# Sums of w_out's blocks put together by transfers instead of VectorE additions

## The chip, the cores and the metric

One Trainium2 chip, one of its cores. The metric is the device time of one execution in microseconds, the median of the runs of one kernel. The core has five engines that run side by side, each through its own list of instructions in order: TensorE (PE; its weight loads are shown as PEld), VectorE (DVE), ScalarE (ACT), GpSimd (POOL) and SyncE (SP), which here only issues transfers. Engines wait for each other by semaphores. Transfers are carried out by 16 DMA engines.

## The reference

Linear attention for 8 batches of 8 heads, 576 tokens, 64 columns a head, and then a feed-forward layer with softplus, on 4608 tokens of 512 columns and 2048 hidden columns, in float32:

```
q_s = exp(q - max(q, -1));  q_s = q_s / (sum(q_s, -1) + 1e-9)
k_s = exp(k - max(k, 2));   k_s = k_s / (sum(k_s, 2) + 1e-9)
kv  = einsum('bhsd,bhse->bhde', k_s, v)
x   = einsum('bhsd,bhde->bhse', q_s, kv)      # heads side by side: 4608 x 512
h   = x @ w_in
g   = maximum(h, 0) + log1p(exp(-abs(h)))
out = g @ w_out
```

## The kernel before, in words

Tokens come in nine tiles of 512. The hidden columns come in 16 chunks of 128; chunk j holds 128 columns of w_in and the 128 rows of w_out that go with them. TensorE multiplies in a reduced float32, so each operand is kept as a high part and a low part and a product takes three matmuls (high by high, low by high, high by low). A chunk with both parts of both matrices is 1 MB in SBUF (`parts[j]`, lines 198 to 207); it is stored once to DRAM (`keep_w`) and fetched again where it is needed.

Tiles 0 to 2 are multiplied plainly, chunk by chunk: `up` (lines 595 to 597) makes 512 columns of h, ScalarE bends them, VectorE makes the low part of g (line 613), and `down` (lines 637 to 639) adds to the output. For tile 2 the 16 chunks are fetched one by one by `fetch_w` (line 224) into five buffers in turn (w0, spare, w2, w3, w15), each fetch released when TensorE has left the buffer's former chunk. Tiles 3 to 8 are multiplied in three pairs by a scheme of seven block products in place of eight. It needs sums and differences of blocks of w_in and w_out for each of eight pairs of chunks s = 0 to 7 (chunks 2s and 2s+1). Those of w_out are made by `sum_out_unit(s)` (lines 273 to 299), while tile 2 is being multiplied. Its first two steps, `whole_w(0)` and `whole_w(1)`, put a chunk's high and low part together again, 128 partitions by 512 columns each; steps 2 to 5 form the four combinations (line 283), steps 6 and 7 split them into high and low parts, step 8 stores 1 MB to DRAM.

In the same stretch of time the attention for later tiles goes on: per batch and group of heads the tile `kvt` with k and v is loaded by SP (lines 314 and 318) after GpSimd has set its edges (lines 310 to 313); VectorE takes the maximum along the tokens (line 336), GpSimd the maximum over the partitions (line 339), VectorE subtracts it (line 371), ScalarE takes the exponential, TensorE multiplies k and v (line 387). For a tile of q, VectorE makes the low part `q_lo` (line 529), which the products of lines 535 to 537 wait for.

The order of all work is written out by hand: `ORDER` is a list of short names, `do` carries out one after another, and each engine gets its instructions in that order. `y2.0` is step 0 of `sum_out_unit(2)`, `R0.4` fetches chunk 4, `n` loads the next k and v tile, `U36` and `O36` are up and down of tile 2 for chunk 4 (36 = 2 x 16 + 4). SP takes nearly all transfers, in one queue.

Of the kernel before, what the change touches and what calls it, by code (L numbers as in the profile page):

```python
# [16 lines left out]
ALU = mybir.AluOpType  # L17
# [31 lines left out]

STAGE = ("w1", "w15", "w0", "spare", "w5", "w6", "w7", "w8")  # L50
STAGE_OUT = ("w12", "w13", "w14", "w1", "w12", "w13", "x1", "w3")
ORDER = """
# [17 lines left out]
def tile_attn_ffn(  # L70
# [9 lines left out]
    nc = tc.nc  # L80
# [162 lines left out]
    def sum_unit(s):  # L243


        f = wp.tile([P, 2, 4, 2 * P], F32R, name=STAGE[s])
        y = f[:, 1].bitcast(F32)
# [25 lines left out]
    def sum_out_unit(s):  # L273

        f = (xp if STAGE_OUT[s][0] == "x" else wp).tile([P, 2, 4, 2 * P], F32R, name=STAGE_OUT[s])
        y = f[:, 1].bitcast(F32)

        def whole_w(z, engine=nc.vector):
            hi, lo = (parts[2 * s + z][:, i, 1].bitcast(F32) for i in range(2))
            engine.tensor_tensor(out=y[:, 2 * z:2 * z + 2].rearrange("p a n -> p (a n)"), in0=hi, in1=lo, op=ALU.add)  # L280

        def add(out, a, b, op, engine=nc.vector):
            engine.tensor_tensor(out=y[:, out], in0=y[:, a], in1=y[:, b], op=op)

        def high():
            nc.scalar.copy(f[:, 0], y)

        def low():
            nc.vector.tensor_tensor(out=f[:, 1], in0=y, in1=f[:, 0].bitcast(F32), op=ALU.subtract)

        def keep():
            kept_sums_out[s] = dram.tile([P, 2, 4, 2 * P], F32, name=f"sums_out{s}")
            nc.sync.dma_start(out=kept_sums_out[s], in_=f.bitcast(F32))

        return [
            lambda *e: whole_w(0, *e), lambda *e: whole_w(1, *e), lambda *e: add(3, 1, 3, ALU.add, *e),
            lambda *e: add(1, 0, 1, ALU.subtract, *e), lambda *e: add(0, 3, 0, ALU.subtract, *e),
            lambda *e: add(2, 2, 0, ALU.subtract, *e), high, low, keep,
        ]
# [797 lines left out]
```

## Time and profile before

| | us |
|---|---|
| median of 3 runs | 813.59 (813.24 to 814.54) |
| span of the profiled execution, first to last instruction | 811.1 |
| TensorE busy | 800.8 |
| VectorE busy | 625.9 |
| ScalarE busy | 536.3 |
| GpSimd busy | 115.1 |
| DMA queue of SP, share of the 16 engines' span | 67.3% |

The profile comes from one execution; of its time the page gives the span. "Busy" is the time in which an engine executes; its waits, and what released it, are listed apart. Shares over the whole span are averages over stages with different limits, so the rows below are taken from the stretch of time in which the changed instructions stand.

### The profile page before, as it was taken

To read this page: it belongs to the slowest core of one execution; us is meant where nothing else is said; L and a number is where in the kernel's file an instruction comes from. 1 tells how busy PE (TensorE), PEld (TensorE's weight loads), DVE (VectorE), ACT (ScalarE), POOL (GpSimd) and SP (SyncE) were. 2 spreads that over 40 slices of the span, in tenths; PEclk is the share of its full clock that TensorE was granted. 3 is DMA by queue.
4 is the path that set the end of the run, shared out by engine and by line. 5 is a ranking of instruction groups with operands and counts; after the bars stand their busy time and mean duration, and the time that the engine had idled before them with its cause. 6 is when DMAs were issued, how large, how long until landed. Compare 5 with 4: busy or idle time off the path is not lost.

```text
span 811.1 us, 12147 instructions
## 1 busy us (share of the span) xinstructions
PE 800.8 (99%) x4244; PEld 656.6 (81%) x4244; DVE 625.9 (77%) x1027; ACT 536.3 (66%) x868; POOL 115.1 (14%) x219
## 2 busy tenths in 40 slices
PE   8999999999999999999999999999999999999997
PEld 7578888888877888888888888888888888888886
DVE  8888974569989999767889998767999922237983
ACT  4999974646777575778885765978657544445651
POOL 2320022000010100010100003440001350000044
PEclk9999999999999999999999999999999999999999
DMA  9974116749987998998497637982866695449654
GB/s 340 373 273 182 59 39 274 267 176 385 401 279 257 328 337 343 340 372 253 139 324 237 186 115 265 275 270 93 280 201 197 178 261 198 175 156 322 211 126 70
DMA packets 114493, 193.75 MB, mean 239 GB/s; under 512 B 8000, under 2 KB 90176, under 8 KB 104192
## 3 DMA queue, kind: packets, MB, share of 16 engines
q1 hardware_dynamic: 111168, 186.67, 67.3%
q0 software_dynamic: 2944, 6.04, 4.0%
q8 instruction: 34, 0.56, 0.3%
q10 hardware_dynamic: 320, 0.26, 0.1%
q14 instruction: 27, 0.22, 0.1%
HBM read 149.95 MB, written 42.99 MB: 238 GB/s over the span
## 4 chain that ended last, share of the span: by engine, by line
PE 92%; DVE 3%; issue 2%; DMA 2%; SPq 1%; ACT 0%; POOL 0%; DVEq 0%; ACTq 0%; POOLq 0%
PE po L722 6%; PE po L838 6%; PE po L836 6%; PE po L837 6%; PE po L724 6%; PE po L723 6%; PE ph L595 5%; PE po L637 5%; PE ph L597 5%; PE ph L596 5%; PE po L638 5%; PE po L639 5%; PE ph L722 3%; PE ph L724 3%; PE ph L723 3%; PE ph L836 3%
## 5 line engine op out<-in xcount | busy, mean ns | idle before, releaser
L881 POOL DMA_DIRECT2D out<-w x92 | 59.3, 653 | 305.7 <-DVE w L873 304.4
L816 ACT CAST g_hi<-w 128x512 fp32r<-128x512 f32 x74 | 46.2, 624 | 31.1 <-PE ph L837 8.0
L595 PE MATMUL ph<-x,w 128*128 128x512 f32 x164 | 65.3, 398 | 1.1 <-DMA w<-kept 1.1
L637 PE MATMUL po<-w,g_hi 128*128 128x512 f32 x164 | 64.5, 394 | 0.0
L596 PE MATMUL ph<-x,w 128*128 128x512 f32 x164 | 64.0, 390 | 0.0
L597 PE MATMUL ph<-x,w 128*128 128x512 f32 x164 | 64.0, 390 | 0.0
L639 PE MATMUL po<-w,g_lo 128*128 128x512 f32 x164 | 64.0, 390 | 0.0
L638 PE MATMUL po<-w,g_hi 128*128 128x512 f32 x164 | 63.9, 390 | 0.0
L819 DVE TENSOR_TENSOR g_lo<-w,g_hi 128x512 fp32r<-128x512 f32 x74 | 51.0, 690 | 16.0 <-ACT g_hi L816 12.6
L803 DVE TENSOR_TENSOR w<-w,w 128x512 f32<-128x512 f32 x72 | 49.2, 686 | 5.3 <-ACT w L756 5.2
L752 ACT ACTIVATE w<-w 128x512 f32<-128x512 f32 x48 | 30.1, 632 | 34.8 <-DVE w L745 18.9
L745 DVE TENSOR_TENSOR w<-po,w 128x512 f32<-128x512 f32 x24 | 16.6, 690 | 46.9 <-PE po L724 46.3
L816 ACT CAST w<-w 128x512 fp32r<-128x512 f32 x52 | 32.2, 623 | 25.1 <-DVE w L819 8.1
L604 ACT ACTIVATE g<-ph 128x512 f32<-128x512 f32 x48 | 28.6, 599 | 29.8 <-PE ph L597 26.7
L722 PE MATMUL po<-w,x 128*128 128x512 f32 x112 | 44.1, 394 | 0.0
L724 PE MATMUL po<-w,x 128*128 128x512 f32 x112 | 43.7, 390 | 0.0
L723 PE MATMUL po<-w,x 128*128 128x512 f32 x112 | 43.7, 390 | 0.0
L610 ACT CAST g_hi<-g 128x512 fp32r<-128x512 f32 x46 | 28.6, 621 | 21.2 <-PE po L638 20.7
L613 DVE TENSOR_TENSOR g_lo<-g,g_hi 128x512 fp32r<-128x512 f32 x46 | 31.4, 683 | 12.6 <-ACT g_hi L610 12.4
L339 POOL PARTITION_ALL_REDUCE mx<-mx x20 | 17.2, 860 | 160.6 <-DVE mx L336 133.0
L336 DVE TENSOR_REDUCE mx<-kvt 128x128 f32<-128x640 f32 x28 | 36.9, 1319 | 2.5 <-DMA kvt<-in_kv_tail 2.5
L819 DVE TENSOR_TENSOR w<-w,w 128x512 fp32r<-128x512 f32 x52 | 35.6, 689 | 3.1 <-ACT w L816 1.0
(392 smaller groups left out, 2381.8 us busy)
## 6 DMA issues: line engine op xcount, KB each, us to landing
x<-sums SPq DMA_DIRECT2D x24, 1024.0 KB, 5.2
kvt<-in_kv SPq DMA_DIRECT2D x30, 512.0 KB, 7.4
kept<-w SPq DMA_DIRECT2D x15, 1024.0 KB, 9.6
w<-kept SPq DMA_DIRECT2D x13, 1024.0 KB, 8.1
x<-sums_out SPq DMA_DIRECT2D x44, 256.0 KB, 4.9
w<-kept SPq DMA_DIRECT2D x36, 256.0 KB, 4.5
x<-kept SPq DMA_DIRECT2D x36, 256.0 KB, 4.5
w<-sums_out SPq DMA_DIRECT2D x36, 256.0 KB, 5.6
```

The source lines that it names most:

```text
L595: nc.tensor.matmul(ph, lhsT=w_hi, rhs=x_hi, start=h == 0, stop=False)
L596: nc.tensor.matmul(ph, lhsT=w_lo, rhs=x_hi, start=False, stop=False)
L597: nc.tensor.matmul(ph, lhsT=w_hi, rhs=x_lo, start=False, stop=h == HP - 1)
L637: nc.tensor.matmul(po, lhsT=g_hi[:, ms], rhs=w_hi, start=j == 0, stop=False)
L638: nc.tensor.matmul(po, lhsT=g_hi[:, ms], rhs=w_lo, start=False, stop=False)
L639: nc.tensor.matmul(po, lhsT=g_lo[:, ms], rhs=w_hi, start=False, stop=j == NJ - 1)
L722: nc.tensor.matmul(ph, lhsT=w_hi, rhs=x_hi, start=c == 0 and i in (0, 4), stop=False, **more)
L723: nc.tensor.matmul(ph, lhsT=w_lo, rhs=x_hi, start=False, stop=False, **more)
L724: nc.tensor.matmul(ph, lhsT=w_hi, rhs=x_lo, start=False, stop=c == 1, **more)
L816: nc.scalar.copy(ring[p, i, s][0], right_of(p, i, s))
L819: engine.tensor_tensor(out=lo, in0=right_of(p, i, s), in1=hi.bitcast(F32), op=ALU.subtract)
L836: nc.tensor.matmul(bank, lhsT=w_hi, rhs=hi, start=begin, stop=False, **more)
```

## The change

For s = 2 to 5 the two steps `whole_w(0)` and `whole_w(1)` no longer give VectorE an addition. SP issues a transfer that copies the high part (256 KB, from SBUF to SBUF) into the target, and GpSimd issues a transfer that adds the low part to it. The four pairs are s = 2, 3, 4 and 5, so eight additions of line 280 become eight copies and eight adding transfers. `ORDER` is the same. Lines behind line 50 have a number larger by 1 in the kernel after, and those behind the function's changed lines one larger by 6 (line 224 becomes 225, 280 becomes 286, 339 becomes 345).

```diff
 STAGE = ("w1", "w15", "w0", "spare", "w5", "w6", "w7", "w8")
+BY_DMA = (2, 3, 4, 5)
...
         def whole_w(z, engine=nc.vector):
             hi, lo = (parts[2 * s + z][:, i, 1].bitcast(F32) for i in range(2))
-            engine.tensor_tensor(out=y[:, 2 * z:2 * z + 2].rearrange("p a n -> p (a n)"), in0=hi, in1=lo, op=ALU.add)
+            total = y[:, 2 * z:2 * z + 2].rearrange("p a n -> p (a n)")
+            if s in BY_DMA:
+                nc.sync.dma_start(out=total, in_=hi)
+                nc.gpsimd.dma_start(out=total, in_=lo, accum_op=ALU.add)
+                return
+            engine.tensor_tensor(out=total, in0=hi, in1=lo, op=ALU.add)
```

SP's queue before, around the fetch of chunk 11 (`spare<-kept`); `sums` are stores of w_in's combinations, the fetch into `w_2755` is chunk 12, that into `w_2830` chunk 13:

```order
L265 DMA sums_2687<-w_1960 128x2048
L224 DMA spare<-kept_1876 128x2048
L265 DMA sums_2732<-w_1989 128x2048
L224 DMA w_2755<-kept_1904 128x2048
L314 DMA kvt<-in_kv 128x8x128
L318 DMA kvt<-in_kv_tail 64x2x128
L224 DMA w_2830<-kept_1664 128x2048
```

The same place after; `w_2712` is the target of pair 5, its first copy reads chunk 10 (`w_2645`) and its second chunk 11:

```order
L266 DMA sums_2693<-w_1960 128x2048
L283 DMA w_2712<-w_2645 128x512
L225 DMA spare<-kept_1876 128x2048
L266 DMA sums_2739<-w_1989 128x2048
L225 DMA w_2762<-kept_1904 128x2048
L283 DMA w_2712<-spare 128x512
L320 DMA kvt<-in_kv 128x8x128
L324 DMA kvt<-in_kv_tail 64x2x128
L225 DMA w_2838<-kept_1664 128x2048
```

The first copy of pair 5 stands ahead of the fetch of chunk 11, and the second ahead of the load of the next k and v tile and the fetch of chunk 13.

GpSimd before, where the edges of a k and v tile are set and two maxima over the partitions follow:

```order
L313 MEMSET kvt 128x10
L310 MEMSET kvt 64x2x64
L311 MEMSET kvt 64x2x65
L313 MEMSET kvt 128x10
L339 ISA mx<-mx 128x128 x2
```

GpSimd after, at the same place; the transfers are the adding ones of pair 2 (its second) and of pair 3 (its first):

```order
L284 DMA w_2284<-w_2297 128x512
L316 MEMSET kvt 64x2x64
L317 MEMSET kvt 64x2x65
L319 MEMSET kvt 128x10
L345 ISA mx<-mx 128x128
L284 DMA w_2430<-spare 128x512
L345 ISA mx<-mx 128x128
```

An adding transfer, which waits for its copy, now stands ahead of the tile's edges and of each of the two maxima.

GpSimd before, at the last maximum of this stretch:

```order
L313 MEMSET kvt 128x10
L339 ISA mx<-mx 128x128
L310 MEMSET kvt 64x2x64
L311 MEMSET kvt 64x2x65
L313 MEMSET kvt 128x10
```

GpSimd after, at the same place, with the last three adding transfers (of chunks 9, 10 and 11):

```order
L284 DMA w_2620<-w_2546 128x512
L284 DMA w_2712<-w_2645 128x512
L345 ISA mx<-mx 128x128
L284 DMA w_2712<-spare 128x512
L316 MEMSET kvt 64x2x64
L317 MEMSET kvt 64x2x65
L319 MEMSET kvt 128x10
```

Two of them stand ahead of the maximum, and the last one between it and the edges of the k and v tile that is loaded next.

## Rows read from the trace of the kernel before

**Rows 1.** The page: the span, and busy time of each engine
```profile
span 811.1 us, 12147 instructions
PE 800.8 (99%) x4244; PEld 656.6 (81%) x4244; DVE 625.9 (77%) x1027; ACT 536.3 (66%) x868; POOL 115.1 (14%) x219
```

**Rows 2.** TensorE's waits from 225 to 330 us: who for, us, times, longest
```profile
PE ph L595 <- DMA w<-kept: 1.1, 1, 1.1
PE att L535 <- DVE q_lo L529: 0.7, 1, 0.7
```

**Rows 3.** Busy time by stretch: PE, PEld, DVE, ACT, POOL, clock, DMA share, GB/s
```profile
240.00:262.00 22.00, 21.29 (x127) 17.50 (x124) 21.73 (x39) 17.46 (x32) 2.34 (x8) 1.00 0.76 245
262.00:290.00 28.00, 28.00 (x192) 22.83 (x192) 27.12 (x54) 17.61 (x28) 3.82 (x13) 1.00 0.95 341
290.00:314.00 24.00, 24.00 (x119) 20.32 (x118) 23.24 (x41) 18.13 (x32) 0.25 (x2) 1.00 0.98 348
314.00:340.00 26.00, 26.00 (x116) 21.55 (x115) 23.57 (x39) 15.66 (x25) 1.80 (x2) 1.00 0.85 309
```

**Rows 4.** Order of time on SP's queue: start, us, line, operation, target and source
```profile
239.63 0.33 SPq L224 DMA_DIRECT2D w<-kept  x1
243.89 0.33 SPq L224 DMA_DIRECT2D spare<-kept  x1
277.58 0.38 SPq L224 DMA_DIRECT2D spare<-kept  x1
289.15 0.55 SPq L314 DMA_DIRECT2D kvt<-in_kv  x1
303.37 0.56 SPq L224 DMA_DIRECT2D w<-kept  x1
```

**Rows 5.** Transfers issued at 239.63, 243.89, 277.58 and 303.37: KB each, us to landing
```profile
w<-kept SPq DMA_DIRECT2D x1, 1024.0 KB, 5.4
spare<-kept SPq DMA_DIRECT2D x1, 1024.0 KB, 6.4
spare<-kept SPq DMA_DIRECT2D x1, 1024.0 KB, 8.9
w<-kept SPq DMA_DIRECT2D x1, 1024.0 KB, 10.5
```

**Rows 6.** Order of time on TensorE at three places
```profile
256.25 0.36 PE L535 MATMUL att<-q_hi,kv_hi 128*128 128x192 f32 x1 [0.71 <-DVE q_lo L529]
289.50 0.50 PE L595 MATMUL ph<-x,spare 128*128 128x512 f32 x1
314.25 0.39 PE L595 MATMUL ph<-x,w 128*128 128x512 f32 x1
```

**Rows 7.** Line 280: duration ns least, median, most; first and last start
```profile
L280 DVE TENSOR_TENSOR w<-w x11: 628/686/693, 218.0 to 321.1; 128x512 f32<-128x512 f32 x11
```

**Rows 8.** Order of time on VectorE near 253 us
```profile
252.45 0.82 DVE L371 TENSOR_TENSOR kvt<-kvt,mx 128x640 f32<-128x640 f32 x1
253.79 0.68 DVE L280 TENSOR_TENSOR w<-spare 128x512 f32<-128x512 f32 x1
```

**Rows 9.** Line 881, GpSimd's transfers of 64 KB: duration ns
```profile
L881 POOL DMA_DIRECT2D out<-w x92: 648/648/974, 494.1 to 805.0; - x92
```

**Rows 10.** Order of time on GpSimd at two places
```profile
250.78 0.70 POOL L339 PARTITION_ALL_REDUCE mx<-mx  x1 [9.13 <-DVE mx L336]
289.20 0.20 POOL L310 MEMSET kvt<- 64x128 f32 x1 [5.76 <-ACT w L679]
```

**Rows 11.** Transfers from 262 to 314 us, GB/s in 40 slices; tails from 200 to 335
```profile
GB/s 277 403 240 334 365 337 126 338 403 246 378 339 360 404 353 347 290 334 429 441 422 231 273 246 341 355 332 390 391 315 309 246 378 447 429 429 410 388 320 361
DMA packets 7162, 17.88 MB, mean 344 GB/s; under 512 B 369, under 2 KB 4977, under 8 KB 5367
kvt<-in_kv_tail SPq DMA_DIRECT2D x8, 64.0 KB, 6.9
```

**Rows 12.** Transfers issued from 320 to 340 us
```profile
out<-w SPq DMA_DIRECT2D x4, 256.0 KB, 2.6
```

## The prediction

> **What bounds the kernel now.** I read the page first, then the waits of TensorE, then busy time by stretch, then the order of time on each engine around the changed instructions, and last the transfers. TensorE is busy 99% of a span of 811.1 us [rows 1], so an edit on another engine counts only where TensorE has to wait. Between 225 and 330 us, the stretch in which the sums of w_out's blocks are formed, it waited twice: 1.1 us for a chunk of weights and 0.7 us for VectorE's q_lo [rows 2]. The reader should then see how little room each helper has there. VectorE works 21.73 of 22 us, then 27.12 of 28 and 23.24 of 24; the 16 DMA engines have a share of 0.76 before 262 us, 0.95 until 290 and 0.98 until 314 [rows 3]. So two resources are nearly full beside a TensorE that is full: the change relieves one and loads the other.
>
> What links the DMA engines to TensorE is the stream of weight chunks for the third tile of tokens (the 16 fetches of line 224). The fetch of chunk 15 is issued at 303.37 [rows 4] and lands 10.5 us later [rows 5], at 313.87; TensorE takes the chunk at 314.25 [rows 6]. That is 0.4 us in hand. For chunk 11 the same views give 277.58 + 8.9 = 286.5 against 289.50, so 3.0 us. Chunk 15 is the tightest of the sixteen behind the changed instructions.
>
> **What goes from VectorE.** Eight additions, the 128x512 ones of line 280 that start between 241 and 287 us, at 0.686 us each [rows 7]; consecutive ones start 0.6 us apart, so 4.8 us of VectorE's time. It hides almost wholly, since TensorE waits for VectorE only at 256.25, for 0.71 us [rows 6]. Three removed additions stand before the q_lo it waits for, the last at 253.79 [rows 8], so the stall could vanish: at best -0.7 us. After 262 no wait is left to remove.
>
> **What comes to GpSimd.** Eight accumulating transfers, each standing in GpSimd's order where VectorE's addition stood. GpSimd's transfers cost it 0.65 us each [rows 9], 5 us in all; GpSimd is mostly idle. But each waits until its copy has landed, and behind it on the same engine stand the maxima over the partitions (line 339) and the clearing of the next k and v tile. Take the one before the maximum at 250.78 [rows 10]. Its copy waits for chunk 5, issued at 239.63 [rows 4] and landed 5.4 us later [rows 5], at 245.0; a copy more ahead of it makes that about 246. By then the fetch of chunk 6 is queued (issued 243.89), which landed after 6.4 us, at 250.3, and now lands about 1.2 later with a copy and an addition more ahead of it. Transfers of one queue land in their order here: a 64 KB tail takes 6.9 us [rows 11], longer than 256 KB behind little else, 2.6 us [rows 12]. So the copy lands near 252.3, the addition is issued, the clearing and the maximum (0.7 us) follow, and VectorE's subtraction, at 252.45 before [rows 8], starts near 254.3: 1.9 late, 1.3 after the 0.6 saved at 253.79. The q_lo comes 1.3 later and the stall becomes 2.0, not 0. This delay is not added below: a TensorE 1.3 us late at 256 still meets the same late weights at 314.
>
> **What comes to the DMA engines.** Sixteen transfers of 256 KB, two for each addition, 4.2 MB. The trace before has no copy from SBUF to SBUF and no adding transfer, so I bound the price. From 262 to 314 us 17.88 MB moved [rows 11] in about 50.1 us of busy share, 2.8 us per MB or 0.73 us for 262,144 bytes; the best slice there, 447 GB/s, gives 0.59. An adding transfer reads its target as well as its source, so at most twice 0.73. I take 0.65 for both kinds, between the two rates, because these are runs of 2 KB, and 4,977 of the 7,162 packets behind the mean are shorter. The ends stay 0.59 and, for the adding ones, 1.46.
>
> The Trainium skill (DMA: Bandwidth & Descriptors, "Rules for kernel authors") says of an accumulating transfer that it "reads its destination and writes it later". No row before shows one; by the rule the upper end, +10.1, gains weight.
>
> Which of the sixteen matter? Five (the copies of the first three additions and the first two adding transfers) fall before 262, where 0.24 of 22 us, 5.3 us, is free: absorbed. Eleven come after, five copies and six adding ones, all ahead of chunk 15 in time: 11 x 0.65 = 7.2 us. Free there: 0.05 x 28 + 0.02 x 24 = 1.9 us. With the 0.4 that chunk 15 has in hand, TensorE meets it late by 7.2 - 1.9 - 0.4 = 4.9 us. With the cheapest price and the adding transfers free of charge it is 5 x 0.59 - 2.3 = +0.7; with the dearest 5 x 0.73 + 6 x 1.46 - 2.3 = +10.1.
>
> The Trainium skill (DMA: Bandwidth & Descriptors, "Issuing engines are not separate DMA queues") states that transfers from all issuing engines run on the same 16 DMA engines. No transfer of GpSimd's falls into this stretch, so the trace is silent; by the rule all eleven count, and without it the adding ones might not: 5 x 0.65 - 2.3 = +1.0.
>
> **What comes to SP's queue.** Each copy also waits there for its chunk. The copy of chunk 10 now stands ahead of the fetch of chunk 11 and holds it until chunk 10 has landed: an estimate of 1 to 3 us after the 277.58 of before, against 3.0 in hand. This is part of the same lateness, not one more term.
>
> After 314 nothing gives the time back: TensorE is busy 26.00 of 26 us to 340 [rows 3], and later fetches are released by its own progress. So span 811.1 + 4.9 = 816.0. The profiled execution's span is 2.5 us under the median of the runs, 813.59; I take the same 2.5 around it: 818.5 us.
>
> **Rivals.**
> First, the cover holds, and it is not slower. For: chunk 11 has 3.0 us in hand, a VectorE that is ahead stores its sums earlier and clears the queue before chunk 15, and the transfers might overlap better than a mean rate says. It decides if the eleven transfers cost under 0.35 us each (11 x 0.35 - 2.3 = 1.6). Against: the share is 0.98 from 290 to 314. Time: 811.1 + 2.5 less 0.7 to plus 1.6, that is 812.9 to 815.2.
>
> Second, a convoy on GpSimd and SP in place of the DMA rate. The last copy waits for chunk 11 (288 to 290 by the shift above), lands behind chunk 12 at 293 to 295, its addition and then the clearing of the k and v tile follow (289.20 before [rows 10]), the load of that tile waits for the clearing, and chunk 13's fetch stands behind that load on SP. From that load (289.15 [rows 4]) to chunk 15's landing took 24.7 us at a share of 0.98, so a load at 295 to 297 puts the landing at 320 to 322: +6 to +8, 819.6 to 821.6. For: the order. Against: the late lulls let the queue catch up.
>
> Third, adding transfers at the double price: +10.1, 823.7. For: the addition must fetch two operands. Against: nothing shows that the engine's rate falls with it.
>
> Fourth, VectorE was a bound after all and the stall at 256 vanishes with no cost elsewhere: 812.9. A gain beyond 0.2% of 813.6, 1.6 us (which is also about what a measurement tells from no change), has no wait to come from: after 225 only 1.8 us of waits exist, and the larger, for weights, is not VectorE's.
>
> **How the numbers follow.** DMA rate, +2.5 to +6: 0.47. Convoy: 0.18. Double price: 0.07. Cover holds, within 1.6 us either way: 0.24. Faster by more: 0.04. So slower is 0.47 + 0.18 + 0.07 = 0.72, no change 0.24, faster 0.04. The likeliest case has its own range 816.1 to 819.6. The range to hold the time 8 times in 10 leaves out the double price, half of the convoy and the faster end: 812.9 to 822.
>
> **What would show it.** Right: new waits of TensorE at line 595 for the fetched chunks 11 to 15, the largest near 314 us; a DMA share at 1 from 262 on; 16 more transfers of 256 KB; VectorE waiting at its subtraction for GpSimd's maximum near 252. Wrong: fetches that land as before with chunk 15 in time (the price per transfer was far lower), or TensorE waiting for VectorE or for the product of k and v more than for weights (the convoy on GpSimd decides, not the rate).

## The result, and the profile after

The kernel after takes 825.33 us (median of 4 runs, 825.03 to 826.23), the kernel before, run beside it, 814.07 (813.24 to 814.95). The ratio is 1.0138 with a 95% interval of 1.0123 to 1.0152: 11.2 us slower, where +4.9 and 818.5 us were forecast and 822.0 was the end of the range. The direction was right, the size was not. Medians and ratios, here and below, leave out two executions far off all others, 1002.84 us of pair2 and 1633.52 us of the kernel before beside it.

The page after, against [rows 1]: the span is 12.3 us longer with the same matmuls, and the clock row, 9 from end to end before, has one slice at 8.

```profile
span 823.4 us, 12180 instructions
PE 806.1 (98%) x4244; PEld 660.2 (80%) x4244; DVE 621.3 (75%) x1019; ACT 536.7 (65%) x868; POOL 120.4 (15%) x227
PEclk9999999999999989999999999999999999999999
```

TensorE's waits from 225 to 330 us after, against [rows 2] (us, times, longest):

```profile
PE att L541 <- DVE q_lo L535: 7.5, 2, 4.0
PE att L393 <- ACT kvt L383: 1.9, 1, 1.9
PE ph L601 <- DMA w<-kept: 0.6, 1, 0.6
```

Before there were 1.8 us of waits, now there are 10.0. The wait for weights in these lists says nothing of the change. It stands at 233.89 us before (1.08) and at 233.20 us after (0.56), ahead of the first changed instruction:

```profile
233.89 0.47 PE L595 MATMUL ph<-x,w 128*128 128x512 f32 x1 [1.08 <-DMA w<-kept]
```

Behind it TensorE waits for no weights in either kernel, though the forecast rested on such a wait; what is new is q_lo and the exponentials of k. Busy time by stretch after, against [rows 3] (PE, PEld, DVE, ACT, POOL, granted clock, DMA share, GB/s), and then the two stretches that follow the long waits:

```profile
240.00:262.00 22.00, 18.05 (x86) 14.78 (x81) 17.03 (x30) 14.38 (x26) 5.22 (x11) 0.95 1.00 316
262.00:290.00 28.00, 28.00 (x159) 22.93 (x159) 20.51 (x37) 16.38 (x24) 4.25 (x10) 0.98 0.88 289
290.00:314.00 24.00, 18.56 (x108) 14.89 (x107) 17.41 (x38) 12.66 (x21) 3.38 (x9) 0.86 1.04 333
314.00:340.00 26.00, 26.00 (x122) 21.77 (x121) 24.87 (x44) 15.45 (x27) 0.00 (x0) 1.00 0.87 326
...
259.60:263.40 3.80, 3.80 (x12) 3.01 (x11) 3.80 (x7) 2.90 (x5) 0.70 (x1) 0.55 0.56 139
304.80:311.00 6.20, 6.16 (x18) 5.12 (x19) 6.19 (x9) 2.59 (x5) 1.83 (x7) 0.51 1.08 325
```

The loss stands in two places, 254 to 264 us and 292 to 311 us. After the two long waits for q_lo (the rows below) TensorE ran on at a granted clock of about half (the 1.2 of its two levels, 1.2 and 2.4 GHz): 3.80 x 0.45 + 6.20 x 0.49 = 4.7 us. With 10.0 - 1.8 = 8.2 us of waits that is 12.9, against 12.3 of the span. The same can be read from single rows of TensorE (start, us):

```profile
258.77 0.36 PE L541 MATMUL att<-q_hi,kv_hi 128*128 128x192 f32 x1 [3.95 <-DVE q_lo L535]
...
259.65 0.57 PE L601 MATMUL ph<-x,spare 128*128 128x512 f32 x1
260.01 0.63 PE L602 MATMUL ph<-x,spare 128*128 128x512 f32 x1
...
294.71 0.80 PE L393 MATMUL att<-kvt 128*64 128x65 f32 x20 [1.85 <-ACT kvt L383]
...
304.84 0.58 PE L541 MATMUL att<-q_hi,kv_hi 128*128 128x256 f32 x1 [3.50 <-DVE q_lo L535]
```

The wait of [rows 6] has grown from 0.71 to 3.95, and the matmuls behind it take 0.63 us where one took 0.39. Who was late is read backwards, first on VectorE, then on GpSimd, then on SP and its transfer. VectorE:

```profile
255.57 0.83 DVE L377 TENSOR_TENSOR kvt<-kvt,mx 128x640 f32<-128x640 f32 x1 [4.67 <-POOL mx L345]
258.04 0.68 DVE L535 TENSOR_TENSOR q_lo<-att,q_hi 128x512 fp32r<-128x512 f32 x1
293.05 0.83 DVE L377 TENSOR_TENSOR kvt<-kvt,mx 128x640 f32<-128x640 f32 x1 [2.78 <-POOL mx L345]
298.76 1.43 DVE L289 TENSOR_TENSOR w<-w 128x256 f32<-128x256 f32 x4 [1.93 <-DMA w<-w]
304.10 0.69 DVE L535 TENSOR_TENSOR q_lo<-att,q_hi 128x512 fp32r<-128x512 f32 x1
```

GpSimd, at the same two places (against [rows 10]):

```profile
253.43 0.86 POOL L284 DMA_DIRECT2D w<-w  x1 [9.28 <-ACT w L553]
...
254.82 0.71 POOL L345 PARTITION_ALL_REDUCE mx<-mx  x1
...
291.47 0.86 POOL L284 DMA_DIRECT2D w<-w  x1 [3.63 <-DMA w<-w]
292.05 0.97 POOL L345 PARTITION_ALL_REDUCE mx<-mx  x1
```

And SP, with the copy that the addition of 253.43 waited for, and the load of k and v that was at 289.15 in [rows 4]; the copy landed 7.8 us after its issue, at 252.9:

```profile
245.11 0.51 SPq L283 DMA_DIRECT2D w<-w  x1
296.22 0.71 SPq L320 DMA_DIRECT2D kvt<-in_kv  x1
```

```profile
w<-w SPq DMA_DIRECT2D x1, 256.0 KB, 7.8
```

So the chain at 254 us is: copy lands (252.9), GpSimd issues the addition (253.43), clears a tile, takes the maximum (254.82), VectorE subtracts it (255.57) and, two operations later, makes q_lo (258.04), and TensorE goes on at 258.77. The profile names ScalarE as the releaser at 253.43; but the addition starts 0.5 us after its copy has landed, as the others do (0.3 to 0.6), and the same one in pair2, at 254.07 there, is put down to the copy. At 292 us the same happens once more: TensorE waits 1.85 us for the exponentials of k, VectorE waits at 298.76 for the landing of an addition as well, its q_lo comes at 304.10, and TensorE goes on at 304.84. None of this is given back. Matched matmul by matmul with the trace before, TensorE is 3.9 us late from 260 to 285 us (times of the kernel before), 12.7 from 300 us on, and 12.7 at its last one.

### The profile page after: what moved, and what is told of

It reads as the page before. It is cut to its first block, busy times and chain, and to the rows that moved or that the text cites. A ratio compares the mean times of both kernels' runs of the same rounds, so it can differ in the third digit from the quotient of the medians.

```text
span 823.4 us, 12180 instructions
## 1 busy us (share of the span) xinstructions
PE 806.1 (98%) x4244; PEld 660.2 (80%) x4244; DVE 621.3 (75%) x1019; ACT 536.7 (65%) x868; POOL 120.4 (15%) x227
## 4 chain that ended last, share of the span: by engine, by line
PE 89%; DMA 5%; issue 3%; DVE 2%; SPq 1%; POOL 0%; ACT 0%; POOLq 0%; DVEq 0%
PE po L844 7%; PE po L842 7%; PE po L843 6%; PE po L728 6%; PE po L730 6%; PE po L729 6%; PE ph L601 4%; PE ph L602 4%; PE ph L603 4%; PE po L643 4%; PE po L644 4%; PE po L645 4%; PE ph L728 3%; PE ph L729 3%; PE ph L730 3%; DMA w<-w 3%
## 5 line engine op out<-in xcount | busy, mean ns | idle before, releaser
L601 PE MATMUL ph<-x,w 128*128 128x512 f32 x164 | 66.1, 403 | 0.6 <-DMA w<-kept 0.6
L602 PE MATMUL ph<-x,w 128*128 128x512 f32 x164 | 64.8, 395 | 0.0
L603 PE MATMUL ph<-x,w 128*128 128x512 f32 x164 | 64.6, 394 | 0.0
L619 DVE TENSOR_TENSOR g_lo<-g,g_hi 128x512 fp32r<-128x512 f32 x46 | 31.4, 682 | 12.7 <-ACT g_hi L616 12.5
L601 PEld LDWEIGHTS ph<-x,w 128*128 128x128 f32 x164 | 31.4, 191 | 7.7 <-issue 1.0
```

The lines of the kernel that those rows point to most:

```text
L601: nc.tensor.matmul(ph, lhsT=w_hi, rhs=x_hi, start=h == 0, stop=False)
L602: nc.tensor.matmul(ph, lhsT=w_lo, rhs=x_hi, start=False, stop=False)
L603: nc.tensor.matmul(ph, lhsT=w_hi, rhs=x_lo, start=False, stop=h == HP - 1)
```

## The experiments

My theory from the trace: a convoy on GpSimd, whose additions wait for a landing ahead of the maxima. The rivals: the rate of the transfer engines (the bytes), and adding as such being dear. Each kernel was timed in rounds beside the kernel before. "+2.8 us" is the ratio's distance from 1 times 814 us; the intervals of the ratios are 0.0011 to 0.0018 to each side, 0.9 to 1.5 us, so that a difference of two versions is good to between 1.3 and 2 us.

**One pair at a time** (four kernels, `BY_DMA = (2,)` and so on):

```diff
-BY_DMA = (2, 3, 4, 5)
+BY_DMA = (2,)        # pair3: (3,), pair4: (4,), pair5: (5,)
```

> Only chunks 4 and 5 (pair 2) are summed by transfers; the other three pairs stay on VectorE. Convoy theory (GpSimd stands in its queue waiting for a copy to land, behind it the maximum over partitions of the next head, behind that VectorE and q_lo, and TensorE stalls and then runs at the lower granted clock): pair 2 owns the first stall of the changed kernel (TensorE 3.95 us idle before 258.77 against 0.71 before, then about 1.7 us lost at granted clock 0.50), so +4 to +6 us over before, i.e. 818 to 820 us, with one TensorE wait of 3 to 4 us for q_lo near 254 to 259 and none over 1 us near 292 to 305. Rate theory (16 more transfers on full DMA engines cost in proportion, +12.3 us in all): 4 transfers of 16, +3 us or less (this pair lies in the stretch where the engines were least full), spread as waits for weights, 814.5 to 817 us.

> Only chunks 6 and 7 (pair 3) are summed by transfers. Convoy theory: in the changed kernel neither of this pair's adding transfers stood ahead of a late maximum (the maximum at 260.13 waited for VectorE, the one after 269.30 came 12 us later), so -0.5 to +1 us, 813.5 to 815 us. Rate theory: 4 of 16 transfers in the full stretch, +3 us or more, about 817 us.

> Only chunks 8 and 9 (pair 4) are summed by transfers. Convoy theory: this pair's first add stood ahead of the maximum at 282.10, and its second landed 11.7 us after its issue, so that VectorE waited 1.9 us for it at 298.76; alone it should show +0 to +3 us, 814 to 817 us, the wait being VectorE's for the landing. Rate theory: 4 of 16, about +3 us, 817 us, as waits of TensorE for weights. The two come close here in time and differ in which wait is seen.

> Only chunks 10 and 11 (pair 5) are summed by transfers. Convoy theory: its first add stood at 291.47 ahead of the maximum at 292.05 (VectorE waited 2.78 us for it, TensorE 1.85 us for the exponentials of k), so +1 to +5 us, 815 to 819 us, with the wait of TensorE near 292 to 305 for k's product or q_lo. Rate theory: about +3 us, 817 us, as waits for weights of chunk 13 to 15.

| | us | ratio, interval | |
|---|---|---|---|
| pair2 | 818.88 | 1.0052, 1.0039 to 1.0066 | +4.2 |
| pair3 | 817.18 | 1.0035, 1.0022 to 1.0049 | +2.8 |
| pair4 | 819.57 | 1.0064, 1.0050 to 1.0078 | +5.2 |
| pair5 | 816.03 | 1.0025, 1.0013 to 1.0037 | +2.0 |

The sum, 14.2, is 3 us above the 11.2 of all four, hardly more than the noise of such a sum (about 2.5). Pairs 2 and 5 came out as the convoy theory had it. Pair 3 was a miss for the convoy theory: I had read from the kernel after that none of its additions stood ahead of a late maximum, but alone one does. Pair 4 was a miss for both theories (817 us at most): alone its first addition held the maximum up for 4.76 us, in the kernel after for 2.79. GpSimd and VectorE of pair3:

```profile
257.14 1.17 POOL L284 DMA_DIRECT2D w<-spare  x1 [6.12 <-DVE att L525]
258.07 0.95 POOL L345 PARTITION_ALL_REDUCE mx<-mx  x1
```

```profile
259.06 0.83 DVE L377 TENSOR_TENSOR kvt<-kvt,mx 128x640 f32<-128x640 f32 x1 [1.49 <-POOL mx L345]
```

VectorE's wait for the maximum is there in each of the others too: 5.04 us in pair2 (near 256), 4.76 in pair4 (280), 2.69 in pair5 (285):

```profile
256.20 0.83 DVE L377 TENSOR_TENSOR kvt<-kvt,mx 128x640 f32<-128x640 f32 x1 [5.04 <-POOL mx L345]
```

```profile
280.50 0.83 DVE L377 TENSOR_TENSOR kvt<-kvt,mx 128x640 f32<-128x640 f32 x1 [4.76 <-POOL mx L345]
```

```profile
285.30 0.83 DVE L377 TENSOR_TENSOR kvt<-kvt,mx 128x640 f32<-128x640 f32 x1 [2.69 <-POOL mx L345]
```

A delay that stands at 260 us alone, in pair2, is still there at the end. TensorE's first matmul after it is the row below; matched with the trace before, TensorE is 6.1 us late at 266 us and 6.1 us late at its last matmul (one execution of each kernel, whose spans are 6.6 us apart; over all executions the ratio gives 4.2).

```profile
260.01 0.53 PE L541 MATMUL att<-q_hi,kv_hi 128*128 128x192 f32 x1 [5.06 <-DVE q_lo L535]
```

**The load without the waits.** VectorE makes the sums, and the 16 transfers go to a part of the tile that is written later.

```diff
-                nc.sync.dma_start(out=total, in_=hi)
-                nc.gpsimd.dma_start(out=total, in_=lo, accum_op=ALU.add)
-                return
+                a, b = (f[:, 0, ...] for c in (z, 1 - z))   # two halves that nobody reads
+                nc.sync.dma_start(out=a, in_=hi)
+                nc.gpsimd.dma_start(out=b, in_=lo)
             engine.tensor_tensor(out=total, in0=hi, in1=lo, op=ALU.add)
```

> VectorE makes all eight sums again, and beside them the same 16 transfers are issued from the same two engines at the same places, as plain copies into a part of the staging tile that is written later, so that no transfer waits for another one's landing and nothing waits for a sum. Convoy theory: the bytes alone cost little, 813.5 to 816.5 us (0 to +2.5), waits of TensorE as before the change plus at most a microsecond or two for weights, clock 1.00 throughout. Rate theory: the load is what costs, +6 to +12 us, 820 to 826 us.

Measured: 817.76 us, ratio 1.0055 (1.0042 to 1.0068), +4.5, between the two expectations: the load costs, but not all. TensorE's waits in it, 225 to 330 us, and the fetch of chunk 11 on SP, which was at 277.58 in [rows 4]:

```profile
PE ph L601 <- DMA spare<-kept: 2.0, 1, 2.0
PE att L541 <- DVE q_lo L535: 1.9, 3, 0.8
PE ph L601 <- DMA w<-kept: 0.4, 1, 0.4
```

```profile
281.62 1.25 SPq L225 DMA_DIRECT2D spare<-kept  x1
```

```profile
291.89 0.50 PE L601 MATMUL ph<-x,spare 128*128 128x512 f32 x1 [2.01 <-DMA spare<-kept]
```

The weights that are late are those of chunk 11, not of chunk 15. Behind this wait, too, the granted clock was 0.50 (293 to 295 us).

**Additions behind the maxima.** The copy stays; the adding transfer gets a name of its own in the written order, behind the next maximum or clearing.

```diff
-                nc.gpsimd.dma_start(out=total, in_=lo, accum_op=ALU.add)
...
+        def fold(z):
+            nc.gpsimd.dma_start(out=y[:, 2 * z:2 * z + 2]..., in_=lo, accum_op=ALU.add)
...
- y2.1 O34 q4.6 x3.1.0 n x3.0.1 k4.0.0 A36
+ y2.1 O34 q4.6 x3.1.0 n x3.0.1 k4.0.0 y2.10 A36
```

> All four pairs by transfers as in the changed kernel, but every adding transfer that stood ahead of a maximum over partitions or of a clearing of kvt is issued behind it (behind the maximum of k4.0.0, k4.1.0 and k4.3.0 or behind the next clearing). Convoy theory: VectorE's waits for the maximum shrink to those of before, the stalls at 254 and 292 go and with them the fall of the clock; what stays is the longer way of each chunk's tile to its next fetch: 814 to 818 us. Rate theory and the theory that the adding transfer itself is dear: the same transfers run, so 822 to 826 us.

Measured: 819.72 us, 1.0074 (1.0058 to 1.0091), +6.0. VectorE's waits in it (225 to 345 us): for the maximum 1.2 us in all, for a landed addition 3.3 once.

```profile
DVE w L288 <- DMA w<-w: 3.3, 1, 3.3
...
DVE kvt L380 <- POOL mx L348: 1.2, 2, 0.6
```

TensorE's longest wait in it is 2.3 us, for chunk 11. The convoy theory was right on the waits and wrong on the rest: 5.2 of 11.2 us went, not nearly all; the time lies between the two expectations.

**Plain copies for the additions**, once in the kernel after (`plain`) and once in add_behind (`add_behind_plain`).

```diff
-                nc.gpsimd.dma_start(out=total, in_=lo, accum_op=ALU.add)
+                nc.gpsimd.dma_start(out=total, in_=lo)
```

> As the changed kernel, but the second transfer of each pair is a plain copy instead of an adding one, so the low part is not added; it still waits for the first one's landing. Convoy theory: the wait in GpSimd's queue is the same, 823 to 826 us. Theory that the adding itself is dear (it reads its destination, so twice the work of a copy): the time falls by a good part of the 12 us, to 820 us or less.

> As add_behind (second transfers issued behind the maxima and clearings), but they are plain copies, so the low part is not added. If the adding only lengthens the wait in GpSimd's queue, it costs nothing here: 819 to 820.5 us, as add_behind. If the adding itself loads the transfer engines or lands later and is missed by those who read the sum or wait for the tile: 816.5 to 818 us, near load_no_wait.

Measured: plain 821.13 us, 1.0090 (1.0077 to 1.0103), +7.3; add_behind_plain 816.31 us, 1.0026 (1.0015 to 1.0037), +2.1. The first lies between its two expectations, the second 0.2 us under its lower one: adding costs of itself. The four corners stand in a square:

| second transfer | ahead of the maxima | behind them | its place costs |
|---|---|---|---|
| adding | +11.2 (the kernel after) | +6.0 | 5.2 |
| plain | +7.3 | +2.1 | 5.2 |
| the adding costs | 3.9 | 3.9 | |

The even square hides an uneven split. How much of each time is lower clock can be estimated from the span and granted clock of every execution, as (1 - clock) x span, less the 0.5 to 0.7 us of the kernel before: about 4.5 us of the +11.2, 1.3 of the +7.3, 1.2 of the +6.0 and 0.1 of the +2.1 (one execution's clock is given to 0.001, 0.8 us). So adding cost chiefly clock ahead of the maxima (3.2 of 3.9) and chiefly other time behind them (2.8 of 3.9). That both come to 3.9 is luck, and each difference has 1.4 to 1.8 us of noise.

The price of adding shows in the profile's line on GpSimd's transfer queue (packets, MB, share of 16 engines). Before, plain, after:

```profile
q0 software_dynamic: 2944, 6.04, 4.0%
```

```profile
q0 software_dynamic: 3584, 8.13, 4.8%
```

```profile
q0 software_dynamic: 4096, 8.13, 5.4%
```

For the same 2.1 MB the plain transfers took 0.048 x 818.8 - 0.040 x 811.1 = 6.9 us of the 16 engines, 0.86 each, in 640 packets; the adding ones 0.054 x 823.4 - 32.4 = 12.0, 1.5 each, in 1,152 packets (the shares are rounded to 0.1, which leaves 0.1 us on each). From 225 to 345 us, where this queue carries nothing else, its shares are 5.0% (plain) and 9.6% (after) of 120 us, which gives the finer 0.75 and 1.44 us each.

**Size and chain apart.** VectorE makes the sums; each transfer moves 128 of 512 columns; the second one writes beside the first (load_quarter), over it and so waits for it (chain_quarter), or adds to it (chain_quarter_add).

```diff
+                nc.sync.dma_start(out=a[:, 0:P], in_=hi[:, 0:P])
+                nc.gpsimd.dma_start(out=b[:, 0:P], in_=lo[:, 0:P])      # load_quarter
+                nc.gpsimd.dma_start(out=a[:, 0:P], in_=lo[:, 0:P])      # chain_quarter; _add: accum_op=ALU.add
```

> As load_no_wait (VectorE makes the sums, 16 transfers into a part of the tile that nobody reads, none waiting for another), but each transfer moves 128 of the 512 columns, 64 KB for 256 KB. The places in SP's and GpSimd's queues and what the transfers wait for there stay. Bytes theory (the 4 us of load_no_wait are the rate of the transfer engines): a quarter of the cost stays, 814.5 to 815.8 us. SP-queue theory (a copy that waits on SP for its chunk to land holds the loads of kvt and the next fetch behind it): 817 to 818.5 us, as load_no_wait.

> As load_quarter, but the second transfer of each pair writes where the first one writes, so GpSimd waits for the first one's landing as in the changed kernel; VectorE makes the sums, 64 KB each. With load_no_wait, plain and load_quarter this is the fourth corner of size and chain. Convoy theory (the wait in GpSimd's queue costs by itself): 2.5 to 4 us more than load_quarter, with VectorE waiting for a maximum over partitions several times. Bytes theory: the wait is short because the transfer is small, at most 1 us more than load_quarter.

> As chain_quarter (64 KB each, second transfer waits for the first, VectorE makes the sums), but the second transfer adds. If the price of adding goes with the bytes, a quarter of 4 us: about 820 us. If it is fixed per transfer (a longer issue on GpSimd): 822 to 823 us.

Measured: load_quarter 813.65 us, 0.9997 (0.9982 to 1.0011); chain_quarter 818.88, 1.0062 (1.0043 to 1.0080); chain_quarter_add 819.51, 1.0067 (1.0051 to 1.0083). So eight copies that wait on SP cost nothing while they are small, and the 4.5 us of load_no_wait go with the bytes (about 1.5 of them at the lower clock). A chain of small transfers costs 5.3 us (0.0065), more than the 2.5 to 4 expected and about what the place cost above. Adding a quarter costs 0.4 with 2 us of noise, which is far from the 3.9 of whole transfers, so it goes with the bytes. The chain in chain_quarter, TensorE and VectorE:

```profile
258.23 0.53 PE L541 MATMUL att<-q_hi,kv_hi 128*128 128x192 f32 x1 [3.20 <-DVE q_lo L535]
```

```profile
254.42 0.83 DVE L377 TENSOR_TENSOR kvt<-kvt,mx 128x640 f32<-128x640 f32 x1 [2.70 <-POOL mx L345]
```

**Away from SP.** load_gpsimd: as load_no_wait, but GpSimd issues all 16, behind the maxima. both_gpsimd: the real work with copy and addition both on GpSimd, the addition one place later, and `y4.2 y4.3` moved behind `y3.7` in the written order.

```diff
-                nc.sync.dma_start(out=total, in_=hi)
...
+        def copy(z):
+            nc.gpsimd.dma_start(out=y[:, 2 * z:2 * z + 2]..., in_=hi)
```

> VectorE makes the sums; the 16 transfers of full size are all issued by GpSimd, at the places behind the maxima (those of add_behind), none by SP, and no transfer waits for another's landing. SP-queue theory: with SP's queue as before the change the cost goes, 813.5 to 815.5 us. Bytes theory: 817 to 819 us, as load_no_wait.

> The changed kernel's work (VectorE makes none of the eight sums) arranged anew: the copy and the adding transfer are both issued by GpSimd, the copy behind a maximum or clearing, the add one such place later, and the two operations of VectorE that read the sum of chunks 8 and 9 come later in its order. If the two queues are the whole cause (GpSimd's and SP's): 813 to 815.5 us. If the bytes and the adding cost by themselves: 817 to 820 us, with waits for weights of chunk 11 or for kvt.

Measured: load_gpsimd 816.16 us, 1.0034 (1.0021 to 1.0046), +2.8, between the two expectations; both_gpsimd 819.95, 1.0074 (1.0057 to 1.0090), +6.0, within its second expectation. In both_gpsimd TensorE no longer waits for q_lo at all, but for weights, because a chunk's buffer is given back only when the late addition has read it. TensorE's waits (225 to 330 us), and those of SP's fetches (235 to 320 us; line 225 whole chunks, line 231 blocks of w_in for the next stage):

```profile
PE ph L607 <- DMA w<-kept: 6.7, 3, 3.1
PE ph L607 <- DMA spare<-kept: 0.5, 1, 0.5
```

```profile
SPq L231 <- DMA w<-spare: 8.7, 1, 8.7
SPq L225 <- DMA w<-w: 4.2, 1, 4.2
```

**GpSimd adds itself**, no transfer; `y2.0.1` in the written order passes GpSimd to the addition.

```diff
-BY_DMA = (2, 3, 4, 5)
+BY_DMA = ()
...
- y2.0 ... y2.1 ...
+ y2.0.1 ... y2.1.1 ...
```

> No transfers: the eight sums are ordinary additions on GpSimd, at the places in its queue where the adding transfers stood. Each takes about 1.2 us there (half of the 2.45 us of 128x1024 before) and waits for nothing but its tile. Convoy theory: without a landing to wait for, a maximum behind it is late by about 1.2 us at most, 813 to 816 us. If the order of GpSimd's queue alone were the cause, whatever the instruction waits for, the stalls would come back and the time be near 820 us or more.

Measured: 839.91 us, 1.0325 (1.0308 to 1.0342), +26 us, far past both expectations (813 to 816, and near 820 or more). One addition takes 1.28 us, as expected, but GpSimd and VectorE of this kernel show

```profile
265.10 1.28 POOL L286 TENSOR_TENSOR w<-spare 128x512 f32<-128x512 f32 x1 [8.23 <-issue]
272.36 0.72 POOL L345 PARTITION_ALL_REDUCE mx<-mx  x1 [5.98 <-issue]
```

```profile
273.11 0.83 DVE L377 TENSOR_TENSOR kvt<-kvt,mx 128x640 f32<-128x640 f32 x1 [10.64 <-POOL mx L345]
```

No version was faster than the kernel before beyond its interval; [rows 2] had left 0.7 us of waits for VectorE to win.

## Why the prediction was wrong, point by point

- **TensorE is the bound, and transfers that go with it are paid.** Right, and so was the direction. One of its own signs of being wrong came true: TensorE waits for VectorE and for the product of k and v, and for no weights.
- **The step that failed: "This delay is not added below: a TensorE 1.3 us late at 256 still meets the same late weights at 314."** The delay is not absorbed. In pair2 it stands alone, a wait of 5.06 us with the lower clock behind it, the kernel is 4.2 us slower, and TensorE stays as late as it was. There was no late chunk to absorb it: the 1.1 us for weights in [rows 2] stand at 233.89, ahead of the changes, and in the kernel after TensorE takes chunk 15 at 326.96, 0.8 us after it has landed (issued at 316.40, 9.8 us). A late TensorE gives its buffers back late (before, SP's fetches waited for it 7 times, 22.6 us in all, from 235 to 320 us), so a delay is passed on to the end, not covered. The prediction used that very fact further on ("later fetches are released by its own progress") and not here. The term left out is worth 5.2 us, the difference between the two places in the square.
- **The size of that delay.** The links were the right ones: the copy landed at 252.9 (forecast 252.3). But the addition took GpSimd 0.86 us for the 0.65 taken from plain 64 KB transfers, 0.5 us passed between landing and issue, and VectorE's subtraction came at 255.57 for 254.3; the wait was 3.95 us, not 2.0. It was looked for at one place; there are three (VectorE waits for the maximum at 255.57, 283.10 and 293.05). And the 4.7 us at the lower granted clock were in no term.
- **Rate of the transfer engines, +4.9.** Right in part. The transfers do make weights late, but those of chunk 11 (2.0 us in load_no_wait, 2.3 in add_behind), not of chunk 15. With GpSimd's order out of the way (add_behind) the cost is +6.0, inside the term's own bounds; that it comes near 4.9 is partly luck, since 1.2 of it is lower clock, which was in no term. The price of 0.65 held for neither kind: an adding transfer takes 1.44 us by the queue's share, just under the upper bound of 1.46, a plain one 0.75. The Trainium skill's sentence (DMA: Bandwidth & Descriptors, "Rules for kernel authors") that an accumulating transfer "reads its destination and writes it later" agrees with it: 1.44 us against 0.75.
- **SP's queue is no term of its own.** Right as far as the order goes: with small transfers it costs nothing (load_quarter, 0.9997). Whether the queue counts with whole ones is open; load_gpsimd, with no copy on SP, is 1.7 us cheaper than load_no_wait, about the noise of the two.
- **The rivals as alternatives.** The convoy was given 0.18 and the rate 0.47, as if one excluded the other. Both happened, and in the square their costs add: 2.1 for the bytes, 3.9 for adding, 5.2 for the place, 11.2 in all. In the trace of the kernel after they overlap in part: chunk 11 landed at 295.52 (issued at 286.12, 9.4 us) and TensorE took it at 295.61, so without the 1.85 us for the exponentials of k it would have waited some 1.8 us for weights instead. The convoy's place was partly right (the load of k and v went out at 296.22, forecast 295 to 297), but it cost through the maximum over the partitions, not through that load.

What stays open: load_no_wait (+4.5) is dearer than add_behind_plain (+2.1). The kernels differ in two things, VectorE's eight additions and the places of GpSimd's transfers, and no run separates these. The clock tells more than half of it: by the estimate above it took 1.5 us of load_no_wait and 0.1 of add_behind_plain, and the 1.0 us that is left is within the noise.

## What to carry to other kernels

A transfer that waits for another one's landing blocks all that stands behind it on the engine that issues it; price it as landing plus issue plus the rest of the chain to the bound engine, and put it behind the urgent work of that engine. A delay of an engine that is busy 99% is absorbed only by a wait whose end does not depend on that engine; buffers that it gives back itself do not count, so such delays are added to each other. When two mechanisms act at different times, forecast their sum, not the likelier one, and add what the bound engine loses at a lower clock behind its waits.

## What the runs showed of the hardware that I had not expected

- An adding transfer of 256 KB from SBUF to SBUF cost GpSimd 0.88 us to issue and 1.44 us of the 16 engines, a plain one 0.55 and 0.75. From issue to landing, with the engines full, the adding ones took 4.5 to 12.1 us.
- After waits of 3.95 and 3.50 us the granted clock was 0.5 for 3.8 us (from 0.8 us behind the end of the wait) and for 6.2 us, which cost 4.7 us beside the 7.5 of the waits. After the wait of 1.85 us near 294 it stayed at 1.00; in load_no_wait it fell to 0.50 behind a wait of 2.01.
- Where GpSimd changed, in pool_add, between an addition of its own and a maximum over the partitions, it stood idle for 5.98 to 9.45 us at six places without waiting for anything that the profile shows (8.23 and 5.98 us above). The trace has an instruction MODIFY_POOL_CONFIG 22 times in pool_add on these two lines, and twice on the line of the maximum before, ahead of the first one. The Trainium skill (GPSIMD Engine Reference, "Instruction dispatch") says that the first call to a freshly loaded kernel pays about 6 us to load its code; the 5.98 agrees, the 8.23 is more; that the idle time is the loading of code is not shown here.
